# Two gate/up tiles change phase, and the sums of the input change engine, in an attention and gated-MLP kernel

## The chip, the cores and the metric

The kernel runs as one program on one core of a Trainium2 chip. The time is device microseconds of that core, lower is better. The core has TensorE (PE: matmuls, PEld: loads of their weights), VectorE (DVE), ScalarE (ACT), GpSimd (POOL) and SyncE (SP, whose queue issues the transfers between HBM and on-chip memory).

## The reference

For x of 2048 tokens by 640 features the result is x + attention(xn) + mlp(xn), where xn is x normalised over its features:

```python
xn = _layernorm(x, axis=-1)
return x + _A_ref(xn, A_wqkv, A_wo) + _B_ref(xn, B_w_gate, B_w_up, B_w_down)

# _A_ref: 32 heads of 20, window of 256 tokens
mask = (idx[:, None] - idx[None, :] >= 0) & (idx[:, None] - idx[None, :] < W)
p = _softmax(jnp.where(mask, q @ k.T * Dh ** -0.5, -1e9))
o = (p @ v) @ wo
# _B_ref: 640 -> 1728 -> 640
h = _gelu(x @ w_gate) * (x @ w_up)
y = h @ w_down
```

gelu is the tanh approximation. All inputs and the result are 32-bit floats.

## The kernel before, in words

The tokens are cut into four chunks of 512 (C), the features into five blocks of 128 (KT), the 1728 inner features of the MLP into 14 tiles (NF), the last of which holds 64 gate and 64 up columns together. Every dense product of 32-bit operands is made of three: each operand is split into a high part rounded for TensorE and a low remainder (names ending in h and l), and high by high, low by high and high by low are added. A 128x512 output over 640 features so takes 15 matmuls of 512 columns (`dense_steps`, L82).

The program has four stages.

1. Normalisation, transposes of x into `xh` and `xl`, and the first projections of q, k and v.
2. The attention, as 32 units of 14 slots each (eight groups of four heads by four chunks). A unit's scores are computed twice: once for the row maxima (matmuls into `ps_m`, L410, reduced on VectorE with the mask added, L412), and later, with the negated maximum as further rows of the product, for the exponentials (matmuls into `ps_e`, L462; ScalarE writes the weights `P`, L464; GpSimd zeroes the masked corners, L470 and L473). The weights come in three banks per unit. One unit later the sum over values follows (matmuls into `ps_o`, L484), which reads all three banks. The negated maxima go by a transfer (`qs` from `mr`, L427) into the rows beside q.
3. The seven-product phase (`gate_up_pair`). For two chunks at a time it computes a whole gate/up tile with sums of weights (`w_sums`) and sums of the input, so that a pair takes 54 matmuls where plain products take 60: 108 a tile against 120.
4. The projection down and the output projection, added to x (matmuls into `ps_w`, L942).

In stage 2 a filler (`filler`, a generator) lends matmuls to the gaps: the projections of q and k for later groups, the values of the second half of the heads, and NFA gate/up tiles (`gate_up_fill`), one matmul at a time. RATE is the number of 512-column matmuls per unit, drawn in equal parts at each slot (`pull_fill`). Before slot 0 a ramp draws 24 x 4 and a gap 16 more. The list `sets` gives the order: q/k tiles and gate/up tiles in turn. V1_SLOT is the slot from which the second half's values are projected, once the current piece of a set is done. A gate/up tile's gelu in the filler goes step by step, one slot apart (`defer`): ScalarE copies and squares, VectorE forms the inner polynomial (L534, L535), ScalarE takes the tanh, VectorE multiplies twice more (L543, L550), and the result is stored to DRAM (`hd`).

The sums of the input that the seven-product phase needs (`x_sums`, `tx`, L613) are made in stage 2 as well: eight groups of ten operations of 128x256 and four stores each (`td`, L616), set at slots 24 + 50 i + 2 j. They share two buffers, so each sum's tile waits for the store of the tile two before.

The orders of TensorE, ScalarE and VectorE in stage 2 are written out by hand (`MANUAL`). Those of GpSimd and of SP's queue are not: there a planner places each instruction by its own estimate of when its operands are ready. In SP's queue each transfer also waits until the eighth before it has landed.

The q/k projections (`save_qk`) leave TensorE through ScalarE and VectorE into `r`, of which there is one buffer, and from there through ScalarE and GpSimd (L204) into `pt` and to DRAM. GpSimd also makes the low parts of the filler's weights (L515) and of the value weights (L239), and presets the value tiles (L249, L250).

Of the kernel before, what the change touches and what calls it, by code (L numbers as in the profile page):

```python
# [12 lines left out]
AF = mybir.ActivationFunctionType  # L13
OP = mybir.AluOpType
# [10 lines left out]
NF = 14  # L25
# [2 lines left out]
NEG = -3.0e38  # L28
QROWS = 122
NS = 14  # L30
RATE = 49.6
V1_SLOT = 169
MXD = 4
NFA = 8
NDA = 2
WARM = 64
XS0, XSN = 24, 50
# [8 lines left out]
def block_kernel(ctx, tc, x, xt, wqk, wv, wo, wgu, wd, wdl, out):  # L46
    nc = tc.nc
# [30 lines left out]
    def dense_steps(ps, wh, wl, rh, rl, nk, cost=1.0):  # L78
        n = 0
        for a, b in ((wh, rh), (wl, rh), (wh, rl)):  # L80
            for k in range(nk):
                nc.tensor.matmul(ps, a(k), b(k), start=n == 0, stop=n == 3 * nk - 1)  # L82
                n += 1
                yield cost
# [89 lines left out]
    def defer(n, fn, *a):  # L174
        if now[0] is None:
            fn(*a)
        else:
            at(now[0] + n, fn, *a)
# [315 lines left out]
    def load_gu(f):  # L494
        raws = []
        for i in range(2 if f < NF - 1 else 1):
            raw = wrp.tile([128, KT, 128], F32, name="wr", tag="wr")
            nc.sync.dma_start(raw, wgu[2 * f + i])
            raws.append(raw)
        return raws  # L500
# [4 lines left out]
    def split_later(pool, bufs, raw):  # L505
        hi = pool.tile([128, KT, 128], F32R, name="wqh", tag="wqh", bufs=bufs)
        lo = pool.tile([128, KT, 128], F32R, name="wql", tag="wql", bufs=bufs)

        def high():
            nc.scalar.activation(hi, raw, AF.Copy)  # L510
            for k in range(KT):
                defer(1 + k, low, k)

        def low(k):
            nc.gpsimd.tensor_tensor(out=lo[:, k], in0=raw[:, k], in1=hi[:, k].bitcast(F32), op=OP.subtract)  # L515

        defer(1, high)
        return hi, lo

    def gate_up_fill(f, ws, c):  # L520
        cs = slice(c * C, (c + 1) * C)
        pss = []
        st = {}

        def c1():
            gs = st["g"] = hp.tile([128, C], F32, name="gs", tag="gs")
            t = st["t"] = hp.tile([128, C], F32, name="he", tag="he", bufs=2)
            nc.scalar.activation(gs, pss[0], AF.Copy)
            nc.scalar.activation(t, pss[0], AF.Square)
            defer(1, c2)  # L530

        def c2():
            gs, t = st["g"], st["t"]
            nc.vector.tensor_scalar(t, t, 0.044715, 1.0, op0=OP.mult, op1=OP.add)  # L534
            nc.vector.tensor_tensor(out=t, in0=gs, in1=t, op=OP.mult)  # L535
            defer(1, c3)

        def c3():
            nc.scalar.activation(st["t"], st["t"], AF.Tanh, scale=math.sqrt(2.0 / math.pi))
            defer(1, c4)  # L540

        def c4():
            nc.vector.scalar_tensor_tensor(st["g"], st["t"], 1.0, st["g"], op0=OP.add, op1=OP.mult)  # L543
            st["done"] = True

        def c5():
            if "done" not in st:
                defer(1, c5)
                return
            nc.vector.scalar_tensor_tensor(st["t"], st["g"], 0.5, pss[1], op0=OP.mult, op1=OP.mult)  # L550
            nc.sync.dma_start(hd[f][c], st["t"])

        for i, (wh, wl) in enumerate(ws):
            ps = psd.tile([128, C], F32, name="ps_d", tag="dn")
            pss.append(ps)
            yield from dense_steps(ps, lambda k: wh[:, k, :], lambda k: wl[:, k, :],
                                   lambda k: xh[:, k, cs], lambda k: xl[:, k, cs], KT)
            defer(1, c5 if i else c1)

    sets = [("qk", 1), ("gu", 0), ("qk", 2), ("gu", 1), ("qk", 3), ("gu", 2), ("qk", 4)]  # L560
    sets += [("gu", f) for f in range(3, NFA)] + [("gu", NF - 1)]
    pools = (wp, None), (hp, 2)
    rest = []

    def filler():
# [6 lines left out]
        for s, (kind, i) in enumerate(sets[:-1]):  # L572
            nxt = []
            after = sets[s + 1]
            for c in range(NC):
# [14 lines left out]
                if c in (1, 2) and c <= len(raws):  # L590
                    nxt.append(split_later(*pools[(s + 1) % 2], raws[c - 1]))
                if pending and now[0] >= V1_SLOT:
                    pending = False
# [8 lines left out]
    def x_sums(p, k, half):  # L602
        w = C // 2
        a, b = (slice((2 * p + i) * C + half * w, (2 * p + i) * C + half * w + w) for i in (0, 1))
        eh, el = xh.bitcast(F32), xl.bitcast(F32)
        live = {}

        def tile_of(i):
            live[i] = ap.tile([128, w], F32, name="tx", tag="tx")
            return live[i]  # L610

        def dve(o, i, j, op):
            nc.vector.tensor_tensor(out=o, in0=i, in1=j, op=op)  # L613

        def store(i):
            nc.sync.dma_start(td[p][i][:, k, half * w:half * w + w], live[i])  # L616

        def s1():
            dve(tile_of(1), eh[:, k, b], eh[:, k, a], OP.subtract)

        def s2():
            dve(live[1], live[1], el[:, k, b], OP.add)

        def s3():
            dve(live[1], live[1], el[:, k, a], OP.subtract)
            store(1)

        def s4():
            dve(tile_of(2), eh[:, k + 2, b], live[1], OP.subtract)

        def s5():
            dve(live[2], live[2], el[:, k + 2, b], OP.add)
            store(2)

        def s6():
            dve(tile_of(4), eh[:, k + 2, a], live[2], OP.subtract)

        def s7():
            dve(live[4], live[4], el[:, k + 2, a], OP.add)
            store(4)  # L640

        def s8():
            dve(tile_of(3), eh[:, k + 2, b], eh[:, k, b], OP.subtract)

        def s9():
            dve(live[3], live[3], el[:, k + 2, b], OP.add)

        def s10():
            dve(live[3], live[3], el[:, k, b], OP.subtract)
            store(3)  # L650

        return s1, s2, s3, s4, s5, s6, s7, s8, s9, s10

    NU = NG * NC
# [4 lines left out]
    def pull_max(n, slot):  # L659
        for _ in range(n):  # L660
            x = next(stream, None)
            if x is None:
                return
            max_piece(*x)
            if x[1] == 15:
                at(slot + MXD, max_end, x[0])
# [4 lines left out]
    def pull_fill(n):  # L671
        debt[0] += n
        while debt[0] > 0:
            debt[0] -= next(fill, 1.0)

    def attention():
# [15 lines left out]
        for u in range(NU + 1):  # L692
            if 1 <= u and u + 2 < NU:
                load_stack(u + 2)
            for i in range(NS):
# [5 lines left out]
                if i % 2 == 0:  # L701
# [3 lines left out]
                    pull_max(3 if i in (6, 12) else 2, T)  # L705
                pull_fill(RATE / NS)
        while acts:
# [77 lines left out]
    def load_xs(p, i):  # L785
        t = cp.tile([128, 2, C], F32, name="ht", tag="ht", bufs=3)
        nc.sync.dma_start(t, td[p][i])
        return t
# [167 lines left out]
    order.__enter__()  # L956
    raws_w = load_gu(NFA)
    xraw = {i: load_xs(0, i) for i in (2, 1, 3)}
# [61 lines left out]

    raws_next = {NFA + 1: load_gu(NFA + 1)}
    for j, f in enumerate(range(NFA, NF - 1)):
        end = f + 1 == NF - 1
# [56 lines left out]
    for n, (c, kind, i) in enumerate(steps):  # L1080
        if (kind, i) == ("d", 0):
            pss = [psn.tile([128, C], F32, name="ps_w", tag="w") for _ in range(KT)]
# [57 lines left out]
```

## Time and profile before

| | |
|---|---|
| median of 3 runs | 1116.48 us (1115.81 to 1116.67) |
| the profiled execution | 1116.69 us |
| its span, first to last instruction | 1115.0 us |
| TensorE busy | 1098.7 us, 99% |
| VectorE busy | 637.7 us, 57% |
| ScalarE busy | 470.9 us, 42% |
| GpSimd busy | 359.9 us, 32% |
| mean granted TensorE clock | 0.995 |

The attention runs from some 92 us to 715 us, the last gate/up tile follows to 729 us, the seven-product phase to 851.7 us, and the last stage takes the rest. A row of a group of instructions reads: line, engine, operation, output from inputs, count, busy time in us, mean ns of one, and the engine's idle time ahead of them with what ended it. In a view in order of time the first two numbers are start and length in us.

### The profile page before, as it was taken

The numbers are of one execution on the slowest core, as the hardware profiler recorded it, in microseconds if no ns is written. First come the engines' busy times: TensorE is split into PE (matmuls) and PEld (weight loads), VectorE is DVE, ScalarE is ACT, GpSimd is POOL, SyncE is SP. The second block draws the span as 40 slices with busy tenths as digits, with TensorE's granted clock in tenths as the row PEclk, the third lists the DMA queues.
The fourth block names the chain that finished last, engine by engine and source line by source line (L and its number), as shares of the span: only waits on it lengthen the run. The fifth ranks groups of instructions, "written<-read, shape, count | busy, mean of one in ns | idle before, by whom it ended". The sixth has DMA issues, their size and how long they took to land.

```text
span 1115.0 us, 19319 instructions
## 1 busy us (share of the span) xinstructions
PE 1098.7 (99%) x6802; PEld 837.6 (75%) x6802; DVE 637.7 (57%) x1736; ACT 470.9 (42%) x952; POOL 359.9 (32%) x504
## 2 busy tenths in 40 slices
PE   7999999999999999999999999999999999999998
PEld 7887666767668876667667676788888878788886
DVE  7856676757648577586777775566664350211203
ACT  4434554555555455645545454643323421211111
POOL 4122542644552233534323343311113313222230
PEclk8999999999999999999999999999999999999999
DMA  4642343543443314343242431342214835152431
GB/s 157 220 143 60 103 144 115 139 146 95 139 144 109 87 58 143 111 146 107 80 140 83 125 104 38 107 150 92 89 66 157 264 125 175 48 179 75 152 95 66
DMA packets 76145, 133.10 MB, mean 119 GB/s; under 512 B 12800, under 2 KB 33664, under 8 KB 76048
## 3 DMA queue, kind: packets, MB, share of 16 engines
q1 hardware_dynamic: 76048, 131.87, 37.6%
q8 instruction: 53, 0.87, 0.3%
q14 instruction: 44, 0.36, 0.1%
HBM read 86.31 MB, written 44.83 MB: 118 GB/s over the span
## 4 chain that ended last, share of the span: by engine, by line
PE 91%; DVE 4%; ACT 1%; DMA 1%; issue 1%; POOL 1%; SPq 0%; DVEq 0%; ACTq 0%; POOLq 0%
PE ps_d L82 28%; PE ps_w L942 23%; PE ps_g L851 11%; PE ps_o L484 7%; PE ps_e L462 7%; PE ps_m L410 6%; PE ps_v L82 6%; DVE junk L412 2%; PE ps_g L82 1%; PE ps_t L156 1%; PE ps_d L296 1%; ACT P L464 1%; PE ps_b L912 0%; DMA xi<-x 0%; DMA qs<-qd 0%
## 5 line engine op out<-in xcount | busy, mean ns | idle before, releaser
L412 DVE CUSTOM_DVE_ANT_0 junk<-ps_m,mask 128x384 bf16<-128x384 f32 (+2 forms) x512 | 271.2, 530 | 158.0 <-PE ps_m L410 120.0
L464 ACT ACTIVATE P<-ps_e 128x512 f32<-128x512 f32 (+2 forms) x384 | 197.5, 568 | 71.0 <-PE ps_e L462 64.6
L470 POOL TENSOR_SCALAR_AFFINE_SELECT P<-P 128x512 f32<-128x512 f32 x128 | 83.8, 655 | 221.1 <-ACT P L464 212.8
L82 PE MATMUL ps_d<-xh,wqh 128*128 128x512 f32 x510 | 150.4, 407 | 0.0
L82 PE MATMUL ps_d<-xh,wql 128*128 128x512 f32 x510 | 150.3, 407 | 0.0
L82 PE MATMUL ps_d<-xl,wqh 128*128 128x512 f32 x510 | 149.3, 406 | 0.0
L410 PE MATMUL ps_m<-ks,qs 120*128 120x128 bf16 (+1 forms) x704 | 120.9, 275 | 4.1 <-DVE mx L412 2.8
L921 POOL TENSOR_TENSOR ht<-hr,ht 128x512 fp32r<-128x512 f32 x52 | 69.2, 1337 | 172.1 <-ACT ht L919 142.9
L462 PE MATMUL ps_e<-qs,ks 122*128 122x128 bf16 (+2 forms) x704 | 112.5, 277 | 0.8 <-ACT P L464 0.6
L82 PEld LDWEIGHTS ps_d<-xl,wqh 128*128 128x128 f32 x510 | 92.9, 188 | 19.2 <-issue 2.4
L82 PEld LDWEIGHTS ps_d<-xh,wql 128*128 128x128 f32 x510 | 93.1, 189 | 18.0 <-issue 0.9
L82 PEld LDWEIGHTS ps_d<-xh,wqh 128*128 128x128 f32 x510 | 92.6, 188 | 17.2 <-ACT xh L164 0.3
L919 ACT ACTIVATE ht<-hr 128x512 fp32r<-128x512 f32 x56 | 35.1, 629 | 132.7 <-PE ps_w L942 80.8
L462 PEld LDWEIGHTS <-ks 122*128 122x128 bf16 x704 | 49.9, 98 | 54.6 <-issue 44.3
L473 POOL TENSOR_SCALAR_AFFINE_SELECT P<-P 128x512 f32<-128x512 f32 x112 | 74.2, 673 | 51.2 <-ACT P L464 51.2
L410 PEld LDWEIGHTS <-qs 120*128 120x128 bf16 x704 | 62.1, 98 | 33.1 <-issue 13.7
L484 PE MATMUL ps_o<-P,v 128*32 128x384 f32 (+2 forms) x1408 | 84.3, 386 | 0.0
L204 POOL TENSOR_TENSOR pt<-r,pt 128x512 bf16<-128x512 f32 x40 | 47.3, 1181 | 105.1 <-ACT pt L203 104.8
L484 PEld LDWEIGHTS ps_o<-P,v 128*32 128x32 f32 x1408 | 40.1, 110 | 39.6 <-issue 32.8
L923 DVE TENSOR_TENSOR ht<-hr,ht 64x512 fp32r<-64x512 f32 x4 | 2.8, 690 | 112.3 <-ACT ht L919 112.3
L515 POOL TENSOR_TENSOR wql<-wr,wqh 128x128 fp32r<-128x128 f32 x115 | 51.6, 481 | 38.0 <-ACT wqh L510 38.0
L488 ACT ACTIVATE ob<-ps_o 128x512 f32<-128x512 f32 x32 | 19.1, 597 | 101.1 <-PE ps_o L484 58.5
(270 smaller groups left out, 1889.2 us busy)
## 6 DMA issues: line engine op xcount, KB each, us to landing
hd<-he SPq DMA_DIRECT2D x52, 256.0 KB
hr<-hd SPq DMA_DIRECT2D x52, 256.0 KB
wr<-wgu SPq DMA_DIRECT2D x27, 320.0 KB
qs<-qd SPq DMA_DIRECT2D x32, 240.0 KB
ks<-kd SPq DMA_DIRECT2D x32, 240.0 KB
xi<-x SPq DMA_DIRECT2D x16, 320.0 KB
qs<-qd SPq DMA_DIRECT2D x32, 160.0 KB
ks<-kd SPq DMA_DIRECT2D x32, 160.0 KB
```

The lines of the kernel that those rows point to most:

```text
L82: nc.tensor.matmul(ps, a(k), b(k), start=n == 0, stop=n == 3 * nk - 1)
L410: nc.tensor.matmul(ps[:, lo:hi], lh, rhs, start=True, stop=True)
L412: nc.vector.tensor_tensor_reduce(out=junk[:, 0:n], in0=ps[:, 0:n], in1=mask[:, 384 - n:384], scale=1.0, scalar=NEG, op0=OP.add, op1=OP.max ...
L462: nc.tensor.matmul(ps[:, col:col + n], k[0:QROWS, j, kc:kc + 128], q[0:QROWS, j, q0:q0 + n], start=True, stop=True)
L464: nc.scalar.activation(pt[:, j, lo:hi], ps[:, lo:hi], AF.Exp, scale=SCALE)
L470: nc.gpsimd.affine_select(out=a, in_=a, pattern=[[0, 4], [1, 128]], compare_op=OP.is_ge, fill=0.0, base=0, channel_multiplier=-1)
L473: nc.gpsimd.affine_select(out=a, in_=a, pattern=[[0, 4], [-1, 128]], compare_op=OP.is_ge, fill=0.0, base=-1, channel_multiplier=1)
L484: nc.tensor.matmul(o[32 * j:32 * j + 32, q0:q0 + n], v[:, w0_:w0_ + 32], pt[:, j, col:col + n], start=i == 0, stop=i == len(todo) - 1, ski ...
L515: nc.gpsimd.tensor_tensor(out=lo[:, k], in0=raw[:, k], in1=hi[:, k].bitcast(F32), op=OP.subtract)
L851: nc.tensor.matmul(ps, i, j, start=first and n == 0, stop=n == len(work) - 1, skip_group_check=True)
L921: nc.gpsimd.tensor_tensor(out=t[:, 1, :], in0=raw, in1=t[:, 0, :].bitcast(F32), op=OP.subtract)
L942: nc.tensor.matmul(pss[m], w[:, ms], r, start=first and j == 0, stop=last and j == len(work) - 1)
```

## The change

- NFA goes from 8 to 6: the filler makes gate/up tiles 0 to 5 and the last one; tiles 6 and 7 are made in the seven-product phase, which makes seven tiles instead of five.
- RATE goes from 49.6 to 42.2, V1_SLOT from 169 to 158, and `sets` orders the q/k and gate/up tiles anew: two q/k tiles follow each other.
- In `x_sums` all ten operations of a group go from VectorE to GpSimd. Their stores stay on SP's queue.
- In the filler's gelu the factor 0.044715 goes into the scale of ScalarE's Square, so that VectorE forms the polynomial in one operation in place of two.

Since the sums' slots bind only the engines with a written order, the planner now places them on GpSimd and their stores in SP's queue. In the built program five of the first group's ten stand ahead of the first mask, five between the second and third bank's masks of unit 0, and the others between the masks of later units up to unit 27.

```diff
-RATE = 49.6
-V1_SLOT = 169
+RATE = 42.2
+V1_SLOT = 158
 MXD = 4
-NFA = 8
+NFA = 6
...
-            nc.scalar.activation(t, pss[0], AF.Square)
+            nc.scalar.activation(t, pss[0], AF.Square, scale=math.sqrt(0.044715))
             defer(1, c2)
 
         def c2():
             gs, t = st["g"], st["t"]
-            nc.vector.tensor_scalar(t, t, 0.044715, 1.0, op0=OP.mult, op1=OP.add)
-            nc.vector.tensor_tensor(out=t, in0=gs, in1=t, op=OP.mult)
+            nc.vector.scalar_tensor_tensor(t, t, 1.0, gs, op0=OP.add, op1=OP.mult)
             defer(1, c3)
...
-    sets = [("qk", 1), ("gu", 0), ("qk", 2), ("gu", 1), ("qk", 3), ("gu", 2), ("qk", 4)]
-    sets += [("gu", f) for f in range(3, NFA)] + [("gu", NF - 1)]
+    sets = [("qk", 1), ("gu", 0), ("qk", 2), ("qk", 3), ("gu", 1), ("qk", 4)]
+    sets += [("gu", f) for f in range(2, NFA)] + [("gu", NF - 1)]
...
-        def dve(o, i, j, op):
-            nc.vector.tensor_tensor(out=o, in0=i, in1=j, op=op)
+        def pool(o, i, j, op):
+            nc.gpsimd.tensor_tensor(out=o, in0=i, in1=j, op=op)
...
         def s1():
-            dve(tile_of(1), eh[:, k, b], eh[:, k, a], OP.subtract)
+            pool(tile_of(1), eh[:, k, b], eh[:, k, a], OP.subtract)
...
```

The steps s2 to s10 change from `dve` to `pool` in the same way.

More of the change, by code (lines that the diff above doesn't have):

```diff
@@ L618, in s1 @@
         def s1():
-            dve(tile_of(1), eh[:, k, b], eh[:, k, a], OP.subtract)
+            pool(tile_of(1), eh[:, k, b], eh[:, k, a], OP.subtract)
         def s2():
-            dve(live[1], live[1], el[:, k, b], OP.add)
+            pool(live[1], live[1], el[:, k, b], OP.add)
         def s3():
-            dve(live[1], live[1], el[:, k, a], OP.subtract)
+            pool(live[1], live[1], el[:, k, a], OP.subtract)
             store(1)
         def s4():
-            dve(tile_of(2), eh[:, k + 2, b], live[1], OP.subtract)
+            pool(tile_of(2), eh[:, k + 2, b], live[1], OP.subtract)
         def s5():
-            dve(live[2], live[2], el[:, k + 2, b], OP.add)
+            pool(live[2], live[2], el[:, k + 2, b], OP.add)
             store(2)
         def s6():
-            dve(tile_of(4), eh[:, k + 2, a], live[2], OP.subtract)
+            pool(tile_of(4), eh[:, k + 2, a], live[2], OP.subtract)
         def s7():
-            dve(live[4], live[4], el[:, k + 2, a], OP.add)
+            pool(live[4], live[4], el[:, k + 2, a], OP.add)
             store(4)
         def s8():
-            dve(tile_of(3), eh[:, k + 2, b], eh[:, k, b], OP.subtract)
+            pool(tile_of(3), eh[:, k + 2, b], eh[:, k, b], OP.subtract)
         def s9():
-            dve(live[3], live[3], el[:, k + 2, b], OP.add)
+            pool(live[3], live[3], el[:, k + 2, b], OP.add)
         def s10():
-            dve(live[3], live[3], el[:, k, b], OP.subtract)
+            pool(live[3], live[3], el[:, k, b], OP.subtract)
             store(3)
```

## The prediction

> **What bounds the kernel now.** I read the page first: its busy table, its slices, its chain.
>
> ```profile
> span 1115.0 us, 19319 instructions
> PE 1098.7 (99%) x6802; PEld 837.6 (75%) x6802; DVE 637.7 (57%) x1736; ACT 470.9 (42%) x952; POOL 359.9 (32%) x504
> PEclk8999999999999999999999999999999999999999
> ...
> PE 91%; DVE 4%; ACT 1%; DMA 1%; issue 1%; POOL 1%; SPq 0%; DVEq 0%; ACTq 0%; POOLq 0%
> ```
>
> TensorE is busy everywhere at the full granted clock and holds 91% of the chain that ended last, VectorE 4%. A busy TensorE can still be stretched, so I looked for the pace of its matmuls, in the chain in order of time (start, length, what):
>
> ```profile
> 578.70 2.08 PE ps_o L484 x32
> ...
> 653.87 1.61 PE ps_d L82 x7
> 655.48 2.08 PE ps_o L484 x32
> ...
> 715.37 13.90 PE ps_g L82 x60
> 729.27 122.40 PE ps_g L851 x540
> 851.67 7.25 PE ps_w L942 x32
> ```
>
> In the filler seven matmuls of 512 columns take 1.61 us, 0.230 each. The seven-product phase runs 540 in 122.40 us without a gap: 0.2267 each, 24.48 us for each of its five tiles. The attention's unit, from one sum over values (ps_o) to the next, is (655.48 - 578.70) / 4 = 19.2 us. The view by stretches says what the other engines have left there:
>
> ```profile
> 578.70:655.48 76.78, 76.77 (x558) 53.64 (x562) 56.31 (x173) 40.54 (x80) 26.22 (x45) 1.00 0.37 111
> ...
> 729.27:851.67 122.40, 122.40 (x542) 101.35 (x541) 79.04 (x135) 41.56 (x75) 18.07 (x12) 1.00 0.27 93
> ```
>
> The columns after the length are PE, weight loads, DVE, ACT, POOL. VectorE is at 73% and GpSimd at 34% of the attention; in the seven-product phase VectorE is at 65%. Last, the order of time where TensorE did wait in the attention:
>
> ```profile
> 497.33 0.42 DVE L613 TENSOR_TENSOR tx<-tx,xl 128x256 f32<-128x256 f32 x1
> ...
> 498.03 0.57 PE L410 MATMUL ps_m<-ks,qs 120*128 120x128 bf16 x3
> ...
> 498.85 0.42 DVE L613 TENSOR_TENSOR tx<-tx,xl 128x256 f32<-128x256 f32 x1
> 498.99 0.32 PE L410 MATMUL ps_m<-ks,qs 120*128 120x384 bf16 x1 [0.39 <-DVE mx L412]
> ```
>
> The score matmul for the row maximum waits for a maximum, and that maximum stood behind input sums (tx) on VectorE. From the start times of the matmuls, some 18 such stops between 111 and 715 us last 0.2 to 0.8 us each, 7.7 us together; 4.3 us of them fall in the eight stretches of 20 slots in which input sums are made.
>
> **The change, part by part.**
>
> **Two tiles move.** The filler loses 2 x 4 chunks x 2 x 15 = 240 matmuls: 240 x 0.230 = 55.2 us (54.4 at the phase's pace). The phase gains 2 x 108 = 216: 216 x 0.2267 = 49.0 us. Net -6.0 us, bounds -5.4 and -6.2. RATE falls with the work: 112 before slot 0 (24 x RAMP 4 + GAP 16) + 32.04 units x 42.2 = 1464, the filler's new total (before, 112 + 32.1 x 49.6 = 1704), so in both it ends in the drain behind the last unit. Per unit TensorE loses 7.4 x 0.230 = 1.7 us: 19.2 becomes 17.5 us. The phase's other engines do the same per tile as in the five shown, where no gap is left; loads and stores per tile stay, at a DMA share of 0.27. The order of the sets and V1_SLOT move with the rate: the second half's value projection starts near slot 167 instead of 176, just ahead of unit 11's value sum, whose end frees its last value tile. I cost this at 0; cover is the three slots (about 3.7 us) to the first copy, against 2.8 us of value sum and 0.4 us of memsets. If it fails, 1 us, once.
>
> **VectorE loses work.** In a unit of gelu filler before: 16 maxima at 0.71 us (starts 251.48 and 252.19) make 11.4, negated maxima 0.28 + 0.51, gelu 1.65 chunks x (0.46 + 0.75 + 0.71 + 0.68) = 4.3: 16.5 of 19.2 us, and inside a sum stretch 7 sums at 0.52 more: 20.2, over the unit. That is where the stops come from. After: 11.4 + 0.8 + 1.41 x (0.71 + 0.71 + 0.68) = 15.2 of 17.5 us, 87% everywhere. The new fused operation is priced by the row of the other one of its form (L543, 710 ns). So the 4.3 us of stops in the sum stretches can go, while the other 3.4 stay since 87% is what 16.5 of 19.2 was. Bounds -4.3 and +2 (shorter slots leave less time after a slot pair with three maxima); I take -2. The factor on the Square costs nothing: same instruction on ScalarE.
>
> **GpSimd gains work.** 80 sums of 128x256. Rows near it:
>
> ```profile
> L204 POOL TENSOR_TENSOR pt<-r,pt 128x512 bf16<-128x512 f32 x40 | 47.3, 1181 | 105.1 <-ACT pt L203 104.8
> L515 POOL TENSOR_TENSOR wql<-wr,wqh 128x128 fp32r<-128x128 f32 x115 | 51.6, 481 | 38.0 <-ACT wqh L510 38.0
> L470 POOL TENSOR_SCALAR_AFFINE_SELECT P<-P 128x512 f32<-128x512 f32 x128 | 83.8, 655 | 221.1 <-ACT P L464 212.8
> ```
>
> Between 481 (128 columns) and 1181 ns (512), by line 0.71 us: 57 us in all, less 20 x 0.48 for two weight tiles that it no longer splits. Its load in the attention goes to about 54%. [...]
>
> What is queued behind a sum: the masks of the weights (L470, L473), which the value sum needs; the low parts of q and k (L204), whose buffer r VectorE needs next; weight splits. Neither GpSimd nor SP is in the written order, so the planner places them: five sums ahead of all masks, five between unit 0's second and third bank, up to five between the banks of units 5, 9, 13, 15, 20, and eight sums with a weight split behind unit 9's last mask. From the trace, the last mask ends 1.5 to 5.0 us (mostly 3.5) before the value sum reads it, and GpSimd idles 2 to 4 us before that mask; two to four sums (1.4 to 2.8 us) fit, five overrun by up to 1 us and eat into the margin. Unit 9's own demand is about 21 us in 17.5, so r may come late there and in unit 10, around 0.5 us each. Each sum also waits for a store of the tile two before it, and these 32 stores sit in SP's queue; the first fourth-sum store stands directly ahead of unit 1's maximum row. SP waits there for a sum due some 2 slots earlier. Bounds 0 and +6; I take +1, near the low end, as the margin is in the trace.
>
> **Sum.** -6.0 - 2 + 1 = -7.0 on the profiled execution's 1116.69 us (span 1115.0, 1.7 around it): 1109.7. The median shown is 0.2 lower; I say 1109.5 us.
>
> **The rivals.**
>
> *VectorE's relief comes in full, GpSimd hides all.* -6.0 - 4.3: 1106.4. For it: the stops cluster in the sum stretches. Against: shorter slots.
>
> *GpSimd late, but not by much.* Behind unit 9, 10, 13, 15, 20 it costs 3 to 6 us: 1112 to 1116. Against: the margins above.
>
> *GpSimd late in most units: slower.* Place: the last mask ahead of each value sum. With a typical margin of 3 us it decides from 3.5 us of delay: 0.5 us lost in some 20 units is 10 us, which takes back 8 and leaves 1118.7; at 1 us it is 1128. For it: margins of 1.5 and 1.7 us exist already (units 26 and 6), and sums wait for store landings. Against: most units hold none to three sums.
>
> *VectorE sets the attention's pace.* Then a unit does not shrink to 17.5. Break-even is 17.5 + 6/32 = 17.7 us; if it stayed at 18.2, the attention would give back 22 us: 1133. Against: the 15.2 us above.
>
> *The two engines block each other.* In the trace a sum on VectorE takes 417 ns alone and 749 ns when mostly beside GpSimd, and the two-operand gelu operation 0.69 and 0.90. After, 110 operations of that kind at most 0.7 us later, with sums running a tenth of the time: 8 us of VectorE spread over 32 units, 0.25 us each of a slack of 2.3. It would take the relief away: 1111.7. [...]
>
> **How the numbers follow.** Main case 0.52 (1107.5 to 1112.5), full relief 0.15, port 0.08, GpSimd somewhat late 0.14, GpSimd late in most units 0.07, VectorE's pace 0.04. The range 1105.0 to 1116.0 leaves out 0.11 and what lies over 1116 of the fourth. 0.2% (2.2 us) is about what a measurement of this kernel can tell from no change: below 1114.3 lie the first three and a third of the fourth, 0.79; within 0.10; above 0.11.
>
> **What the new profile would show.** 756 matmuls of the phase in 171.4 us without a gap, the final gate/up starting near 658 us, units of 17.4 us, no sums on VectorE, 80 on GpSimd at 0.7 to 0.75 us, and value sums that do not wait for masks. I am wrong if units stay over 17.7 us, if the chain goes through GpSimd's masks or r, or if SP's stores hold up the maximum rows.

## The result, and the profile after

| | before | changed |
|---|---|---|
| median of 6 runs each | 1116.58 us (1115.81 to 1117.58) | 1113.09 us (1111.94 to 1113.98) |
| ratio, 95% interval | | 0.9966 (0.9953 to 0.9979) |
| profiled execution, its span | 1116.69, 1115.0 us | 1111.94, 1110.2 us |

The change gains 3.5 us, or 0.34%: the sign was forecast, and half of the 7.0 us. The profiled execution of the changed kernel happens to be the fastest of its six, so the spans differ by 4.8 us and not by 3.5.

The page of the changed kernel, span, busy table, clock and chain:

```profile
span 1110.2 us, 19224 instructions
PE 1091.4 (98%) x6778; PEld 831.3 (75%) x6778; DVE 602.4 (54%) x1646; ACT 469.2 (42%) x952; POOL 411.1 (37%) x568
PEclk9999999999999999999999999999999999999999
...
PE 93%; DVE 3%; DMA 1%; ACT 1%; issue 1%; SPq 0%; POOL 0%; DVEq 0%; ACTq 0%
```

VectorE has lost 35 us and GpSimd has gained 51; TensorE is busy for 7.3 us less, and still bounds nearly everything. Its chain in order of time:

```profile
656.32 2.73 PE ps_o L484 x48
...
660.26 13.89 PE ps_g L82 x60
674.15 171.37 PE ps_g L850 x756
845.53 0.02 issue
...
847.90 4.29 DMA hr<-hd
...
852.92 1.29 POOL ht L920
...
854.26 33.84 PE ps_w L941 x148
```

The 756 matmuls of the seven-product phase take 171.37 us, as forecast (171.4). Between them and the projection down there is something that the chain of before did not have: a load of `hr`, on the path. (Line numbers behind L535 are one lower in kernels with the fused polynomial.)

The two profiled executions, cut at the same instructions:

| us | before | changed | difference |
|---|---|---|---|
| start to the first score matmul | 64.56 | 64.03 | -0.5 |
| attention: from there to the last gate/up tile | 650.81 | 596.23 | -54.6 |
| that tile | 13.74 | 13.73 | 0.0 |
| seven-product phase | 122.40 | 171.36 | +49.0 |
| hand-over: first `ps_w` to first `ps_w<-wd3h` | 10.57 | 11.99 | +1.4 |
| the rest | 252.90 | 252.89 | 0.0 |

The 240 matmuls alone owed the attention 54.4 us at the phase's pace of 0.2267 us (55.2 at 0.230), so almost nothing is left there for VectorE's relief. The view by stretches, from the first to the last sum over values, first of before and then of the changed kernel (length, then PE, weight loads, DVE, ACT, POOL):

```profile
111.44:710.65 599.21, 594.30 (x4354) 421.95 (x4353) 406.80 (x1275) 317.56 (x647) 239.70 (x391) 1.00 0.37 111
```

```profile
109.45:656.25 546.80, 542.36 (x4123) 379.23 (x4123) 345.46 (x1139) 303.42 (x622) 276.53 (x440) 1.00 0.38 114
```

A unit went from 599.21 / 31 = 19.33 us to 546.80 / 31 = 17.64 us (forecast 17.5). VectorE is busy for 68% and then 63% of it, and GpSimd for 40% and 51%.

### The profile page after: what moved, and what is told of

Its sections match the earlier page's. It is cut to its first block, busy times and chain, and to the rows that moved or that the text cites. A ratio compares the mean times of both kernels' runs of the same rounds, so it can differ in the third digit from the quotient of the medians.

```text
span 1110.2 us, 19224 instructions
## 1 busy us (share of the span) xinstructions
PE 1091.4 (98%) x6778; PEld 831.3 (75%) x6778; DVE 602.4 (54%) x1646; ACT 469.2 (42%) x952; POOL 411.1 (37%) x568
## 4 chain that ended last, share of the span: by engine, by line
PE 93%; DVE 3%; DMA 1%; ACT 1%; issue 1%; SPq 0%; POOL 0%; DVEq 0%; ACTq 0%
PE ps_d L82 25%; PE ps_w L941 22%; PE ps_g L850 15%; PE ps_o L484 7%; PE ps_e L462 7%; PE ps_m L410 7%; PE ps_v L82 6%; PE ps_g L82 1%; DVE junk L412 1%; PE ps_t L156 1%; PE ps_d L296 1%; DMA ks<-kd 0%; DMA xi<-x 0%; ACT P L464 0%; PE ps_b L911 0%
## 5 line engine op out<-in xcount | busy, mean ns | idle before, releaser
L82 PE MATMUL ps_d<-xh,wql 128*128 128x512 f32 x430 | 129.2, 410 | 0.0
L82 PE MATMUL ps_d<-xl,wqh 128*128 128x512 f32 x430 | 128.6, 408 | 0.0
L82 PE MATMUL ps_d<-xh,wqh 128*128 128x512 f32 x430 | 128.5, 409 | 0.0
L462 PEld LDWEIGHTS <-ks 122*128 122x128 bf16 x704 | 50.1, 98 | 54.3 <-issue 44.0
L82 PEld LDWEIGHTS ps_d<-xh,wql 128*128 128x128 f32 x430 | 77.9, 189 | 15.5 <-issue 1.9
L82 PEld LDWEIGHTS ps_d<-xl,wqh 128*128 128x128 f32 x430 | 78.2, 188 | 14.8 <-issue 0.4
L82 PEld LDWEIGHTS ps_d<-xh,wqh 128*128 128x128 f32 x430 | 77.8, 189 | 14.1 <-ACT xh L164 0.3
L75 POOL TENSOR_TENSOR wql<-wr,wqh 128x640 fp32r<-128x640 f32 x11 | 17.8, 1626 | 135.8 <-PE ps_g L850 106.1
```

Of the source, the lines that this page charges most:

```text
L462: nc.tensor.matmul(ps[:, col:col + n], k[0:QROWS, j, kc:kc + 128], q[0:QROWS, j, q0:q0 + n], start=True, stop=True)
```

## The experiments

Three edits can be made alone or together: T moves the two tiles (with RATE, V1_SLOT and `sets`), S puts the sums on GpSimd, G fuses the polynomial. Before has none, the changed kernel all three. I call "stops" what the distances between the starts of TensorE's matmuls in the attention exceed the matmul's own time by, where that is over 0.2 us; the matmuls inside a sum over values are left out. This table holds what all the runs below gave; medians are compared with the kernel before on the same chip, and the three columns on the right are from one profiled execution each. The two executions of the changed kernel there differ by 1.4 us in the attention, so a difference of that size between two rows means little.

| run | edits | median us | ratio (95%) | attention us | stops us (count) | hand-over us |
|---|---|---|---|---|---|---|
| before | | 1116.58 | | 650.8 | 7.7 (18) | 10.6 |
| sums only | S | 1117.79 | 1.0009 (1.0001 to 1.0018) | 653.1 | 8.8 (19) | 10.4 |
| gelu only | G | 1113.29 | 0.9973 (0.9962 to 0.9983) | 648.9 | 6.4 (14) | 10.4 |
| sums and gelu | S G | 1112.98 | 0.9968 (0.9956 to 0.9979) | 646.9 | 4.4 (8) | 10.5 |
| tiles only | T | 1123.25 | 1.0060 (1.0048 to 1.0072) | 607.8 | 17.6 (40) | 12.0 |
| tiles and sums | T S | 1118.68 | 1.0026 (1.0016 to 1.0036) | 603.0 | 13.7 (30) | 12.1 |
| tiles and gelu | T G | 1116.61 | 1.0004 (0.9995 to 1.0012) | 601.0 | 11.1 (25) | 12.0 |
| changed | T S G | 1113.09 | 0.9966 (0.9953 to 0.9979) | 596.2 | 7.1 (17) | 12.0 |
| changed, again | T S G | 1113.06 | 0.9968 (0.9956 to 0.9980) | 597.6 | 8.2 (20) | 12.1 |
| changed, WARM 100 | T S G | 1110.23 | 0.9944 (0.9932 to 0.9955) | 596.1 | 6.3 (18) | 10.4 |
| changed, WARM 128 | T S G | 1109.99 | 0.9937 (0.9925 to 0.9949) | 596.1 | 6.1 (17) | 10.4 |
| sums and gelu, WARM 100 | S G | 1112.54 | 0.9961 (0.9949 to 0.9973) | 646.7 | 2.8 (8) | 10.8 |
| before, WARM 41 | | 1117.00 | 1.0001 (0.9992 to 1.0010) | 650.0 | 7.0 (18) | 11.8 |
| changed, sets in turn, WARM 100 | T S G | 1115.37 | 0.9990 (0.9981 to 0.9999) | 601.0 | 11.1 (23) | 10.4 |

The column of the attention runs from the first score matmul to the last gate/up tile. Whole spans of single executions say less, since that matmul starts anywhere between 63.2 and 67.2 us, whatever the edit.

### What stands between the phase and the projection down

> The changed kernel again. In its first profile 1.4 us were lost where the down projection takes over: SP's issue of the load hr<-hd took 2.07 us where its neighbours take 0.40, and it ran at the same time as a 16 KB packet of the instruction queue (at 848.5 us). Theory A, an issue that meets an instruction packet is held, and the packet's place follows from the number of TensorE instructions ahead of it: the same load is held again by 1.5 us or more, TensorE again stands 1.0 to 1.5 us at the hand-over, time 1112.5 to 1113.5. Theory B, an accident of one execution: the issue takes 0.40 us and TensorE does not stand; then 1.4 us below the first profile.

> The changed kernel with 100 warming matmuls at the start in place of 64. They end ahead of the first transpose, so the work after them should start as before; each adds a weight load and a matmul, 72 instructions, so that every later instruction packet of 256 TensorE instructions falls 72 instructions earlier, about 8 us in the dense stages. Theory A: the packet now falls near 840 us, where SP issues nothing; the load hr<-hd at the hand-over is issued in 0.4 us, TensorE stands under 0.3 us there, and the time is 1.0 to 1.5 us below the changed kernel, unless other issues are met in its place. Theory B: no difference in the hand-over.

The first repeats the changed kernel. The second makes TensorE's warming matmuls at the start more, which is meant to move nothing but the place of all later TensorE instructions in its instruction stream:

```diff
-WARM = 64
+WARM = 100
```

The repeat agrees with the first result. With 36 warming matmuls more the kernel takes 1110.23 us, 2.8 us less, where 1.0 to 1.5 were expected, though it has more to do; the first score matmul starts at 64.1 us as before. Where that comes from is seen in SP's queue in order of time, where the loads of `hr` are issued, first in the changed kernel, then with WARM 100:

```profile
847.47 0.32 SPq L886 DMA_DIRECT2D hd<-he  x1
847.90 2.57 SPq L900 DMA_DIRECT2D hr<-hd  x2
850.53 0.42 SPq L731 DMA_DIRECT2D wr<-wd  x1
```

```profile
847.40 0.32 SPq L886 DMA_DIRECT2D hd<-he  x1
847.83 0.89 SPq L900 DMA_DIRECT2D hr<-hd  x2
848.76 0.42 SPq L731 DMA_DIRECT2D wr<-wd  x1
```

Two issues of `hr` take 0.89 us together in the one and 2.57 in the other: single, the second of them takes 2.07 us instead of 0.4. TensorE's order of time in the changed kernel shows what that costs:

```profile
851.92 0.39 PE L941 MATMUL ps_w<-ht,wd1h 128*128 128x512 f32 x1
852.90 0.50 PE L941 MATMUL ps_w<-ht,wd2h 128*128 128x512 f32 x1 [0.59 <-ACT ht L918]
...
854.26 0.73 PE L941 MATMUL ps_w<-ht,wd2h 128*128 128x512 f32 x2 [0.62 <-POOL ht L920]
```

Matmuls here start 0.227 us apart; the two with waits start 0.98 and 1.02 us after the one before, which loses 1.55 us. The issue was held for 1.7 us, and the tiles of the hidden layer that hang on it are late. With WARM 100 the same two follow without a wait. What ran beside the slow issue is in the packets of the trace. The page's table of queues has a row that no line of the program makes (packets, MB, share), in before and after alike:

```profile
q8 instruction: 53, 0.87, 0.3%
```

53 packets of 16 KB; the changed kernel's 6778 matmuls and as many weight loads, 13,556 instructions, divided by 53 are 255.8 each (before, 13,604 and 256.7). By this count, and since the packets move with the warming matmuls, I read them as TensorE's instruction stream in blocks of some 256. TensorE itself lost nothing by them where it runs without a gap: six packets fall into the changed kernel's seven-product phase, and its 756 matmuls still take 171.36 us, no two of them starting over 0.227 us apart. But in the changed kernel one packet runs from 848.5 to 850.1 us, and the issue of `hr` that begins at 848.4 ends right behind it, at 850.5. With WARM 100 that packet lies at 842.0, where no `hr` is issued; in before it lies at 849.3, and its `hr` is issued at 854.1. In the traces of before and of the changed kernel 39 and 60 of SP's 799 issues overlap such a packet. Most of them take no harm (medians 0.56 and 0.39 us, against 0.34 of those that overlap none), but all the issues longer than 1 us, 9 and 13, are among them. In all fourteen traces together it is 128 of 132, while the packets cover some 5% of a span.

> The kernel before with 41 warming matmuls in place of 64: 46 TensorE instructions fewer, so that its instruction packet of 849.3 us comes some 5.2 us later, at about 854.5 us, when SP issues the second load hr<-hd of the hand-over (854.6 us). Theory A (an issue that meets a TensorE instruction packet is held): that load takes 1.5 us or more to issue, and from the first to the thirteenth matmul group of the down projection 12.0 us pass in place of 10.6, in a kernel that has none of the change. Theory B (something of the changed kernel's two more tiles holds it): 0.4 us and 10.6. The time itself: 1116 to 1119, as other issues are met or spared too.

This is the same the other way round: the kernel before, with 23 warming matmuls fewer (WARM 64 to 41), so that its packet moves into the hand-over. The packet went to 853.2 us, and SP's and TensorE's order of time now read

```profile
853.47 2.25 SPq L901 DMA_DIRECT2D hr<-hd  x2
...
858.26 0.50 PE L942 MATMUL ps_w<-ht,wd2h 128*128 128x512 f32 x1 [0.38 <-ACT ht L919]
...
859.62 0.74 PE L942 MATMUL ps_w<-ht,wd2h 128*128 128x512 f32 x2 [0.63 <-POOL ht L921]
```

The held load and its two waits come to the kernel that had neither, and its hand-over goes from 10.57 to 11.79 us. Moved into the hand-over or out of it, the packet takes the held load along. The median hardly moved, though (1117.00 us, ratio 1.0001, 0.9992 to 1.0010): other packets have moved as well, and this trace has 7 long issues where before has 9. So the packet that `hr` met had its price at its place, 1.2 us, and I take the median to show the sum over all places.

> The changed kernel with 128 warming matmuls: a second place of the packets, a further 56 instructions earlier. Theory A: no packet at the hand-over, 10.4 us there as with 100; 1109.5 to 1112, the rest by what the packets meet in the attention. Theory B (100 was luck or helped the start): 12.0 us at the hand-over, 1113.

64 more warming matmuls (WARM 64 to 128): 1109.99 us, the lowest median here, 6.5 us under before (0.9937) and 3.1 under the changed one. Its hand-over is 10.35 us, as with WARM 100 (10.37), so the gain does not hang on one value.

> Both reliefs without the tiles, with 100 warming matmuls. It had no held load at the hand-over with 64, so by theory A there is nothing to win there: within 1.5 us of 1113.0, as the packets meet other issues. By theory B, warming itself is what made the changed kernel faster: 1109.5 to 1110.5.

The check on warming itself: WARM 64 to 100 in the kernel with S and G alone, whose hand-over (10.5 us) had no held load. It gains 0.4 us (1112.98 to 1112.54), less than the intervals resolve. More warming alone does not give the 2.8 us. It is no empty control, though, since here too the packets have moved: in the traces unit 10 (units are counted from 0) takes 20.54 us in place of 22.03, unit 3 takes 20.86 in place of 19.57, and the hand-over takes 10.8 in place of 10.5, with an earlier load of `hr` held for 2.25 us. In unit 3 a store of the input sums takes 2.76 us to issue beside a packet from 166.5 to 168.7 us. SP's queue, GpSimd and TensorE there, with WARM 100:

```profile
166.35 3.24 SPq L615 DMA_DIRECT2D td<-tx  x2
171.48 0.72 POOL L612 TENSOR_TENSOR tx<-xh 128x256 f32<-128x256 f32 x1 [6.04 <-DMA td<-tx]
172.16 0.63 POOL L473 TENSOR_SCALAR_AFFINE_SELECT P<-P 128x512 f32<-128x512 f32 x1
172.85 1.23 PE L484 MATMUL ps_o<-P,v 128*32 128x256 f32 x16 [1.46 <-POOL P L473]
```

The next sum waits for that store to land, the mask stands behind the sum on GpSimd, and the value sum waits for the mask.

Of those 2.8 us the traces show 1.6 in the hand-over (11.99 to 10.37) and 0.7 in unit 8, which takes 18.77 and 18.75 us in the two traces of the changed kernel and 18.08 and 18.11 with WARM 100 and 128: a store of q that takes 1.36 us to issue there, beside a packet (it is shown with the order of the sets below), takes 0.4 us with both. The rest is not placed: the attention as a whole took 596.2 us in one profiled execution of the changed kernel and 597.6 in the other, and 596.1 with WARM 100.

### Which edit gives and which takes

> Of the change only the two tiles, with RATE, V1_SLOT and the order of the sets; sums of the input and the gelu stay as they were on VectorE. Theory A, VectorE's load matters once the unit is short: in a unit of gelu filler inside a sum stretch VectorE then has 11.4 + 0.8 + 1.41 x 2.60 + 3.7 = 19.6 us of work for a unit of 17.5; over some seven such units it falls behind by 2 us each, so the stops grow from 4 to some 12 us and most of the 6 us of saved matmuls is lost: 1115 to 1121. Theory B, VectorE is not on the path: the whole matmul term comes, 1110 to 1113, the same as the changed kernel or better.

> Of the change only the sums of the input on GpSimd. Theory A, the stops of TensorE behind VectorE in the sum stretches (4.3 us) go: 1112.5 to 1115, that is 2 to 4 us below the kernel before. Theory B, as in the changed kernel the stops go there and come again elsewhere (GpSimd late for r and for the masks, transfers held in SP's queue): 1116 to 1118, no gain.

> Of the change only the fused polynomial: 32 operations of 0.46 us less on VectorE, units still 19.2 us long. Theory A, VectorE's relief pays only where the unit is short: within 1.5 us of the kernel before, 1115 to 1118, like the sums alone. Theory B, the relief pays by itself: 2 us or more below, under 1114.5.

> Both reliefs of VectorE, the two tiles not moved. Theory A: the stops behind VectorE in the sum stretches are gone, but in units of 19.2 us they were only 4 us; what GpSimd's sums delay in SP's queue eats some: 1113.5 to 1117. Theory B, relief and tiles add up as separate gains: before to tiles alone is +6.8 us and before to all is -3.4, so the reliefs would be worth 10 us by themselves: 1106 to 1108.

> The changed kernel with the sums back on VectorE. VectorE in a unit of gelu filler inside a sum stretch: 11.4 + 0.8 + 1.41 x 2.1 + 3.7 = 18.9 us for 17.5. Theory A, the excess sets the pace: about 1.4 us in each of some seven such units and some stops beside them, 1118 to 1122. Theory B, the stops of the tiles alone come from the two gelu operations: 1113 to 1115.

> The changed kernel with the two gelu operations unfused. VectorE in a unit of gelu filler: 11.4 + 0.8 + 1.41 x 2.6 = 15.9 of 17.5 us, 91% in place of 87%. Theory A, by excess over the unit: no overrun, 0 to 3 us more than the changed kernel: 1113 to 1116. Theory B, the stops come from the two gelu operations: most of the 10 us comes back, 1118 to 1122.

Each is the kernel before with some of the three edits, whose cores are:

```diff
T:
-RATE = 49.6
+RATE = 42.2
-V1_SLOT = 169
+V1_SLOT = 158
-NFA = 8
+NFA = 6
...
S:
-            nc.vector.tensor_tensor(out=o, in0=i, in1=j, op=op)
+            nc.gpsimd.tensor_tensor(out=o, in0=i, in1=j, op=op)
G:
-            nc.vector.tensor_scalar(t, t, 0.044715, 1.0, op0=OP.mult, op1=OP.add)
-            nc.vector.tensor_tensor(out=t, in0=gs, in1=t, op=OP.mult)
+            nc.vector.scalar_tensor_tensor(t, t, 1.0, gs, op0=OP.add, op1=OP.mult)
```

T holds more than the two tiles: RATE, V1_SLOT and the order of the sets go with it, and no run takes these apart.

The tiles alone make the kernel slower, by 6.8 us against before's median on that chip. Read the column of the attention in pairs with and without T: it should fall by 54.4 us or more each time, and falls by 43.0 with nothing else, by 50.1 beside S, 47.9 beside G and 50.7 beside both. The phase takes 49.0 back and the hand-over 1.4 to 1.7. By these single executions the tiles so cost the kernel 7.4 us, or 0.6, or 2.7, or gain 0.2. By the medians, each against before on its chip, they cost 6.8, 1.0, 3.3 and 0.0, and never bring what was forecast for them. Three of the six runs lie outside both ranges that were set for them: the tiles alone above, tiles and gelu between, sums and gelu between. The other three, S alone, G alone and T with S, came out as the second theory had it. The waits of TensorE (total us, times, longest us) show where the largest part goes, with the tiles alone:

```profile
PE ps_m L410 <- DVE mx L412: 6.1, 18, 0.5
...
PE ps_e L462 <- ACT P L464: 2.1, 3, 1.2
```

In before the first of these is 2.8 us in 8 times:

```profile
PE ps_m L410 <- DVE mx L412: 2.8, 8, 0.4
```

Of the 9.9 us of stops that T adds here, 5.7 stand ahead of score matmuls for the maxima and 3.6 ahead of those for the exponentials (`ps_e`), which stay unexplained. A score matmul needs the buffer that a maximum on VectorE frees. The units got shorter (by 1.7 us in the changed kernel), VectorE's maxima did not (530 ns in the mean before and with the tiles alone), so the maximum is late more often, 18 times in place of 8. One such place of the tiles alone, first in VectorE's order of time, then in TensorE's:

```profile
520.42 0.42 DVE L613 TENSOR_TENSOR tx<-xh,tx 128x256 f32<-128x256 f32 x1
520.76 0.68 DVE L550 SCALAR_TENSOR_TENSOR he<-gs,ps_d 128x512 f32<-128x512 f32 x1
521.35 0.55 DVE L412 CUSTOM_DVE_ANT_0 junk<-ps_m,mask 128x384 bf16<-128x384 f32 x1
```

```profile
521.97 0.32 PE L410 MATMUL ps_m<-ks,qs 120*128 120x384 bf16 x1 [0.54 <-DVE mx L412]
```

An input sum and a gelu operation stand ahead of the maximum, and the matmul starts when the maximum has ended. S takes the sums off VectorE and G one of its four gelu operations a chunk, and with both, in the long units, that wait is all but gone (waits of TensorE with S and G):

```profile
PE ps_m L410 <- DVE mx L412: 0.4, 2, 0.3
```

In the changed kernel, where the units are short, it is back, in the same view:

```profile
PE ps_m L410 <- DVE mx L412: 2.2, 6, 0.7
```

So the tiles use the relief up, by the total of the stops: 7.7 us before, 4.4 with S and G, 7.1 with the tiles besides. It is not the same stops that come back: 2.2 us of the 4.4 are one wait for transfers in unit 10, which is gone in the changed kernel. By medians, S and G without the tiles (1112.98) are as fast as the whole change (1113.09). The theory that relief pays only where units are short falls: it asked for 1113.5 to 1117 us of S and G, and G alone gives 3.0 us in the long units. The theory that relief and tiles simply add up falls too: it asked for 1106 to 1108. The first holds one way round, that the short units need both: with tiles and only one of S and G the kernel is no faster than before, 5.6 us slower than the changed one without G and 3.5 without S.

S alone is a special case: it relieves VectorE and yet its median is 1.4 us higher, a difference that is just resolved (ratio 1.0009, 1.0001 to 1.0018). The attention's loss is above all in unit 10, which takes 23.86 us where before it took 20.43. GpSimd's order of time there, with S alone:

```profile
303.86 0.74 POOL L613 TENSOR_TENSOR tx<-xh,tx 128x256 f32<-128x256 f32 x1
304.68 0.74 POOL L613 TENSOR_TENSOR tx<-tx,xl 128x256 f32<-128x256 f32 x1
...
308.29 1.16 POOL L204 TENSOR_TENSOR pt<-r,pt 128x512 bf16<-128x512 f32 x1
```

and SP's queue behind it, with S alone and then in before:

```profile
309.47 1.30 SPq L210 DMA_DIRECT2D kd<-pt  x3
...
312.08 2.01 SPq L390 DMA_DIRECT2D ks<-kd  x3
```

```profile
308.38 1.30 SPq L210 DMA_DIRECT2D kd<-pt  x3
...
310.99 1.08 SPq L390 DMA_DIRECT2D ks<-kd  x3
```

Two sums put the low part of k (`pt`) back, its store goes out 1.1 us later (1.5 from the start of the unit), the loads of q and k queue behind that store, and one of them is held besides. TensorE's waits with S alone have the end of it:

```profile
PE ps_m L410 <- DMA sd<-ob: 2.4, 1, 2.4
```

This is one stop of 2.4 us, by transfers in one queue. It is not the price of the sums alone: the same matmul of unit 10 stops for 2.2 us with S and G and for 1.7 us with G alone, which has no sum on GpSimd, and both kernels are faster than before, where it stops for 0.6. So what makes S alone slower is only shown in part. A mask was late once with S alone, in unit 3:

```profile
PE ps_o L484 <- POOL P L473: 0.5, 1, 0.5
```

In the changed kernel no value sum waits for a mask: the last one ends 1.15 to 4.1 us ahead of its reader.

### The order of the sets

> The changed kernel with 100 warming matmuls and the sets in turn again (q/k 1, gate/up 0, q/k 2, gate/up 1, q/k 3, q/k 4), V1_SLOT 197. Theory A, two q/k tiles in a row load GpSimd and SP's queue so that transfers come late near unit 8: the stops there go, 1 us below 1110.2. Theory B, the stops only change their places: 1110 to 1113.

```diff
-V1_SLOT = 158
+V1_SLOT = 197
-WARM = 64
+WARM = 100
-    sets = [("qk", 1), ("gu", 0), ("qk", 2), ("qk", 3), ("gu", 1), ("qk", 4)]
+    sets = [("qk", 1), ("gu", 0), ("qk", 2), ("gu", 1), ("qk", 3), ("qk", 4)]
```

This asked whether the stop in unit 8 of the changed kernel, where two q/k tiles follow each other, can simply be ordered away; V1_SLOT had to move with the order. There a store of q (`qd<-pt`) takes 1.36 us to issue at 253.8 us, beside a packet from 253.9 to 254.8 us, and the load of k behind it ends late; the chain in order of time in the changed kernel:

```profile
253.81 1.36 SPq L210
...
257.71 5.28 DMA ks<-kd
...
263.12 0.33 PE ps_m L410 x2
```

With WARM 100 alone the store is no longer held, this stop is gone and the unit takes 18.08 us, so there was little left to win. With the sets in turn it took 17.49 us, but unit 13 grew from 17.57 to 22.02, and the kernel lost 5.1 us against WARM 100 alone (1110.23 to 1115.37), more than either theory allowed. TensorE's waits have the place:

```profile
PE ps_m L410 <- DMA od<-ob: 3.4, 2, 3.1
```

A stop of 3.1 us by transfers came where there had been none. The order of the sets and V1_SLOT so matter by as much as the whole change does.

## Why the prediction was right, and where it was off

The sign and the range (1105.0 to 1116.0) held; the likeliest case (1107.5 to 1112.5 us) was missed by 0.6 us, and 3.5 of the 7.0 us did not come. By the prediction's own steps:

- **Two tiles move, -6.0.** The phase came out at 171.36 us for 171.4, so its +49.0 is right. The attention, from which the 240 matmuls went, fell by 54.6 us with the terms of VectorE and GpSimd included. At the prediction's 0.230 us each the matmuls owed 55.2, at the phase's 0.2267 they owed 54.4. The chain after has both paces (six in a row take 1.39 us, 0.232 each, and twelve take 2.72, 0.227 each), so this term lies within its bounds, -5.4 to -6.2, and the traces do not divide the 54.6 more finely.
- **VectorE loses work, -2 (bounds -4.3 and +2).** Mis-sized. Together with GpSimd's +1 it was to give -1.0, and what is left for the two is 54.4 or 55.2 less 54.6, that is -0.2 to +0.6; the stops went from 7.7 to 7.1 us. Its two halves were each larger than I thought: with S and G alone the stops fall by 3.3 and the attention by 3.9 us, near the upper bound, and with the tiles 2.7 us of stops come back. I had argued from VectorE's share of a unit ("87% is what 16.5 of 19.2 was"). That share was wrong, since I took every maximum at 0.71 us, the distance of two starts; the rows say 531 ns in the mean for a maximum and 82 for reading it out, and the measured shares are 68% and 63%. It was also no measure of stops: the kernel with T and S has VectorE at 64% (356.94 of 555.00 us) and twice the stops of the changed one. The place shown above suggests what does count, how many operations can stand ahead of one maximum within a slot; no run here counts that.
- **The new fused operation, 0.71 us.** It measures 767 ns in 24 of these; the two that it replaces took 0.46 and 0.75, so it relieves VectorE by 0.44 us a chunk. The size was right within 8%. The factor on the Square cost nothing, as forecast: 600 ns before and 601 after.
- **GpSimd gains work, +1.** A sum takes 738 to 768 ns where 0.71 us was read off a line between two rows. Against 418 ns, the mean of the 41 sums of before that ran on VectorE with nothing on GpSimd beside them, that is a ratio of 1.8. The masks kept a margin in the changed kernel, as forecast. What a late GpSimd can cost shows without the tiles, and there the ways that the prediction named do occur: behind a sum that waits for its store a mask comes late, by 0.5 us with S alone and by 1.5 with S, G and WARM 100. The prediction had the low parts of q and k late for the buffer `r`; with S alone they put back the transfers behind them in SP's queue. What of the changed kernel's time is GpSimd's can't be told apart from VectorE's term.

The rows of the sums in the changed kernel (count, busy us, mean ns, idle ahead):

```profile
L612 POOL TENSOR_TENSOR tx<-tx,xl 128x256 f32<-128x256 f32 x48 | 35.8, 748 | 3.1
L612 POOL TENSOR_TENSOR tx<-xh,tx 128x256 f32<-128x256 f32 x16 | 12.3, 768 | 4.4 <-DMA td<-tx 4.1
L612 POOL TENSOR_TENSOR tx<-xh 128x256 f32<-128x256 f32 x16 | 11.8, 738 | 0.0
```

- **What was costed at nothing.** "The phase's other engines do the same per tile" was right for the phase and blind to its end: the hand-over costs 1.4 us in the profiled execution, where a packet of TensorE's instructions (848.5 to 850.1 us) now falls on the load of `hr`. No step of the prediction looked at what the removal of 24 matmuls, and so a shift in the instruction stream, would move. The earlier V1_SLOT was costed at nothing too, and its copies bear that out: TensorE waits for them once, for 0.2 us.
- **The rivals.** VectorE does not set the attention's pace: from the measured 19.33 us the break-even is 19.33 less 49.0 / 32, or 17.80, and a unit takes 17.64. But beside the two reliefs the tiles by themselves no more than break even (1112.98 and 1113.09 us). GpSimd late in most units did not occur. The rival in which the two engines block each other ("port" among the chances) asked for too much; that a port is behind it no run shows. VectorE's operations in the attention, the maxima aside, that start while a sum runs on GpSimd are 1.2 us longer in all than the shortest of their rows (20 operations), where the rival asked for 8; and with the same 80 sums the stops do fall to 4.4 us where the tiles stay.

As a sum: -5.6 in the attention and the phase together (-54.6 and +49.0), where -7.0 was forecast, +1.4 at the hand-over and -0.5 at the start, where executions differ anyway, make -4.7 of the profiled executions' -4.8 us; the medians, -3.5, hold a typical run of the changed kernel, 1.15 us above its profiled one.

So the time came out in the range, but in part by luck: the -6.0 of the tiles was to carry the gain, and the kernel with the two reliefs and without the tiles gains as much. The tiles' saving in matmuls did come, and stops and the hand-over took it back.

Open: why the fused polynomial alone gives 3.0 us by the median, where its trace shows 2.1 from the first score matmul to the end and 1.3 less in stops; why an issue that meets one of TensorE's packets is held, since the traces show only that they coincide and that moving one moves the other; and the 1.15 us between a typical run of the changed kernel and its profiled one. The kernel's second trace, 1.5 us longer than the first, has 0.60 us more in unit 20, with a wait for transfers of 0.8 us, and 0.65 more in unit 27.

## What to carry to other kernels

In this kernel, work taken out of the gaps of a TensorE-bound stage was worth its matmul time less what the move brought back in waits. Look for the operations that can stand ahead of the one awaited, since an engine's share did not tell, and try the relief without the move, since here it gives all of the gain. Before a late transfer is explained by its neighbours, look at when the packets of TensorE's instructions arrive: here they came once in some 256 instructions, 36 more matmuls at the start moved one from 848.5 to 842.0 us, and 64 more (WARM 64 to 128) took 1.6 us out of the hand-over and 3.1 us out of the median. Such an edit can as well move a packet into a worse place, as WARM 41 did in the kernel before (1.2 us at the hand-over) and WARM 100 in unit 3 of the kernel with S and G (1.3 us).

## What the hardware did that was not expected

- An issue of a transfer on SP's queue takes 0.34 us in the median, and some of those that meet a 16 KB packet of TensorE's instruction stream take 1.0 to 2.1 us (2.76 us at most in all traces). The 53 packets come some 17 us apart in the attention and 29 us in the dense stages, and all 22 issues over 1 us in the traces of before and the changed kernel overlap one; in all fourteen traces four issues of 1.04 to 1.43 us do not.
- The place of a packet went with the count of TensorE's instructions, 848.5 us in the changed kernel and 842.0 with WARM 100: all five traces with the two tiles moved and WARM 64 have a hand-over of 11.99 to 12.11 us, and the three with the tiles moved and more warming 10.35 to 10.38.
- A held store reached TensorE by way of GpSimd: in unit 3 of the kernel with S, G and WARM 100 one store held for 2.76 us became 1.46 us of waiting of a value sum.
